# Tokens' sums one chunk sooner, chunk 17's weights ahead of their splits, and the second pair's weight sums later

## The chip, the core and the metric

The kernel runs on one core of one Trainium2 chip. The time is device microseconds of one execution, the median of several runs. TensorE (PE; PEld is its weight load), VectorE (DVE), ScalarE (ACT), GpSimd (POOL) and SyncE (SP, which issues the DMAs) run side by side, each in the order of its own program, and wait for each other at semaphores.

## The reference, cut to what matters

A masked attention feeds a gated mixing block, and that feeds a second mixing block with a channel network. The change lies in the channel network, the last line:

```
x  = attention(q, k, v)                            # 2 x 768 tokens, 512 channels
x  = (u * (w_spatial @ layernorm(v) + b)) @ w_out  # u, v = halves of relu(x @ w_in)
xt = x.transpose(0, 2, 1)
u  = x + (xt @ U @ V).transpose(0, 2, 1)
out = u + relu(u @ w_ch1) @ w_ch2                  # 512 -> 2048 -> 512 channels
```

## The kernel before, in words

Every float32 matrix product is made of three products of rounded halves: a matrix is split in a rounded part (hi) and the rest (lo), and `mm3` (line 238) runs hi x hi, hi x lo, lo x hi. ACT makes hi, POOL or DVE makes lo as source minus hi (`splits`, line 264).

The 2048 hidden channels are 16 chunks of 128. Each chunk is used for two batches of 768 tokens, so there are 32 steps, n = 0 to 31; n = 16 is chunk 0 of batch 1. Chunk n's weights arrive by DMA and are decoded (`ch_decode`, line 841) once, and split again for each use (`ch_split`, line 848) into the tiles wch, in three slots. `m4(n, j)` (line 859) makes the hidden values of half the tokens: 12 matmuls into PSUM bank 0 or 1, then ACT and DVE write them to h as hi and lo, which frees the bank. `m5(n, t)` (line 869) multiplies h by the second weights into the banks 2 to 7, one for each token block; after the last chunk of a batch (n = 15, 31) DVE adds the bank to y and SP sends y out.

For n < 18 one turn of the loop at line 1120 is: 24 matmuls of m4(n), then 18 of m5(n - 1). From n = 18 on, two chunks are taken together in a round of seven products (`m4_seven`, line 977) in place of eight, a Strassen form. It needs sums of token blocks (five of them) and sums of weight blocks (for each pair of chunks):

- `x_sums` (line 913) adds or subtracts blocks of batch 1's tokens: for each of five names and two halves one operation on POOL or DVE and two on DVE, 25 on DVE and 5 on POOL in all. Its results lie in win0, where the DMAs of the chunks' raw weights lay (so the decodes must be over), with bsp as scratch. It is called behind m4(14) (line 1135).
- `x_operands` (line 935) splits these sums into xc: ten roundings on ACT, five subtractions on DVE, five on POOL. Its places held batch 0's tokens, so it is called at n = 16 (line 1123), and its work is forced out at n = 17 (line 1126).
- `w_sums(q)` (line 956) makes pair q's five groups of weight sums and splits them: into wa for even q, into the first halves of wch for odd q.

`m4_seven` runs the products in the order 5, 4, 3, 2, 1, 6, 7 into the banks 0 and 1 in turn. Before a product it forces out the group of weight sums that the product reads, after it come copies and sums on ACT, DVE and POOL (tile tmp), then a share of a list of other steps, mostly m5 of the pair before. In the first round the list holds six m5 of n = 17 and one split of chunk 19's weights.

What fixes the order on the engines is a planner (lines 66 to 190). Work that isn't matrix work is put down as chains of operations (`add`). At each `tick`, called after every three matmuls, the planner goes through the chains in the order in which they were added and emits those operations which, by its own estimate of durations, would start by about the time that TensorE has reached. `flush` emits the rest of the named chains at once, one operation of each in turn. Once emitted, an operation keeps its place on its engine, whatever the true times turn out to be.

Of the kernel before, what the change touches and what calls it, by code (L numbers as in the profile page):

```python
# [28 lines left out]
NCH = 16  # L29
# [36 lines left out]
class Plan:  # L66
# [95 lines left out]
    def tick(self, room=ROOM):  # L162
        now, more, count = self.free["T"], True, dict.fromkeys(LAG, 0)
        while more:
            more = False
            for c in sorted(self.chains, key=lambda c: c.calm):
                key = c.ops[0][0]
                if any(d.ops for d in c.after) or self.free[key] > now + (CALM if c.calm else room):
                    continue
                if self.most and count[key] >= self.most:  # L170
                    continue
                self.probing = 0.0
                c.ops[0][1]()
                start, self.probing = self.probing, None
                if start <= max(now, self.free[key]) + (STALL if room == ROOM else room):
                    count[key] += 1
                    self.emit(c)
                    more = True

    def flush(self, chains):  # L180

        want = list(chains)
        while any(c.ops for c in want):
            for c in [c for c in want if c.ops]:
                first = [d for d in c.after if d.ops]
                if first:
                    want += [d for d in first if d not in want]
                else:
                    self.emit(c)
# [3 lines left out]
def kernel(ctx: ExitStack, tc: tile.TileContext, qk, qt, kn, vab, vn_, gl_,  # L193
# [5 lines left out]
    def program(dense):  # L199
        with tc.tile_pool(name="sb", bufs=1) as sb, \  # L200
                tc.tile_pool(name="ps", bufs=1, space=bass.MemoryType.PSUM) as pp, \
                tc.manual_schedule():
            body(dense, sb, pp)

    def body(dense, sb, pp):
        plan = Plan(nc)
        V, A, G, T, SP = plan.V, plan.A, plan.G, plan.T, plan.SP
        tick, flush = plan.tick, plan.flush
        KEY = {V: "V", A: "A", G: "G", SP: "SP"}

        def tl(tag, n, name):
            t = sb.tile([128, n], F32, tag=tag, name=f"{name}_{int(dense)}")
            plan.home[t.tensor.name] = tag
            return t
# [49 lines left out]
        def splits(hi, lo, src, eh, el):  # L264
            return [o_rnd(eh, hi, src), o_sub(el, lo, src, hi)]
# [390 lines left out]
        P = {}  # L656
# [182 lines left out]
        decoded, split = {}, {}  # L839

        def ch_decode(c):
            f_place(c)
            f, rw = P["f"][c], P["raw"][c % 2]
            ld = plan.add([o_dma(rw.bitcast(I32), w_ch[c].bitcast(I32))], decoded.get(c - 2, []))
            decoded[c] = [plan.add(decode(rw[:, 1024 * j:1024 * j + 1024], f[:, 512 * j:512 * j + 512]), [ld])
                          for j in range(2)]

        def ch_split(n, js=(0, 1)):
            c = seq[n][1]
            w = [t[:, n % 3] for t in P["wch"]]  # L850
            split[n] = [plan.add(splits(w[0][:, 512 * j:512 * j + 512], w[1][:, 512 * j:512 * j + 512],
                                        P["f"][c][:, 512 * j:512 * j + 512], A, G), [decoded[c][j]])
                        for j in js]
# [5 lines left out]
        def m4(n, j, bk):  # L859
            b, c = seq[n]  # L860
            c1, _ = chv(n)
            for k in range(KB):
                mm3(bk[:, 0:384], [c1[l][:, k] for l in range(2)],
                    [X[b][l][:, k, 384 * j:384 * j + 384] for l in range(2)], k == 0, k == KB - 1)
            hi, lo = (P["h1"][n % 2][l][:, 384 * j:384 * j + 384] for l in range(2))
            A.activation(out=r_(hi), in_=bk[:, 0:384], func=AF.Relu)
            V.scalar_tensor_tensor(out=r_(lo), in0=bk[:, 0:384], scalar=0.0, in1=hi, op0=ALU.max, op1=ALU.subtract)
# [15 lines left out]
        def use(n, t, new):  # L883
            if new:
                flush(split[n])
            m5(n, t)
# [3 lines left out]
        SEVEN = NCH + 2  # L890
# [6 lines left out]
        def o_tt(eng, o_, a, b_, op):  # L897
            return KEY[eng], lambda: eng.tensor_tensor(out=o_, in0=a, in1=b_, op=op)
# [36 lines left out]
        def x_operands(two, tmp_):  # L935
            P["xb"] = {"2": [xblock(1, 0, 0)[l] for l in range(2)], "5": [xblock(1, 1, 1)[l] for l in range(2)]}
            places = [t[:, 1536 * n:1536 * n + 1536] for t in (tl("x00", KB * S, "xc0"), tl("x01", KB * S, "xc1"))
                      for n in range(2)] + [tl("uv", 2 * S, "xc2")]
            ready = []
            for p, (c, name) in zip(places, zip(two, ("4", "3", "1", "6", "7"))):  # L940
                hi, lo = (p[:, 768 * l:768 * l + 768].rearrange("p (k t) -> p k t", k=2) for l in range(2))
                P["xb"][name] = [hi, lo]
                ready.append(plan.add([op for k in range(2) for op in splits(hi[:, k], lo[:, k], tmp_[name][k], A, (V, G)[k])],
                                      [c]))
            return ready


        def wblocks(q):
            if q % 2 == 0:
                return [[P["wa"][l][:, 256 * i:256 * i + 256] for i in range(7)] for l in range(2)]  # L950
            return [[P["wch"][l][:, i // 2, 256 * (i % 2):256 * (i % 2) + 256] for i in range(6)]
                    + [P["wa"][l][:, 1792:2048]] for l in range(2)]
# [3 lines left out]
        def w_sums(q, before):  # L956
            n0 = SEVEN + 2 * q
            f0, f1 = (P["f"][seq[n][1]] for n in (n0, n0 + 1))
            a11, a12, a21, a22 = f0[:, 0:256], f0[:, 256:512], f1[:, 0:256], f1[:, 256:512]
            t0, t1_, t2_ = bsp[:, 0:512], P["wk"], bsp[:, 512:768]  # L960
            hi, lo = wblocks(q)

            def two(i):

                return [(wa[:, 256 * i:256 * i + 512] if q % 2 == 0 else wc[:, i // 2, 0:512])
                        for wa, wc in zip(P["wa"], P["wch"])]

            return [plan.add(ops, before[i:i + 1]) for i, ops in enumerate((
                [o_tt(V, t0[:, 0:256], a21, a22, ALU.add), o_tt(V, t0[:, 256:512], a11, a12, ALU.add)]
                + splits(*two(0), t0, A, G),  # L970
                splits(hi[6], lo[6], a22, A, G),
                splits(hi[5], lo[5], a11, A, G),
                [o_tt(V, t1_[:, 0:256], a11, a22, ALU.add), o_tt(V, t1_[:, 256:512], a12, a22, ALU.subtract)]
                + splits(*two(2), t1_, A, G),
                [o_tt(V, t2_, a21, a11, ALU.subtract)] + splits(hi[4], lo[4], t2_, A, G)))]
# [144 lines left out]
        for n in range(1, SEVEN):  # L1120
            if 1 < n and n + 2 < NCH:
                ch_decode(n + 2)
            if n == NCH:
                ready = x_operands(two, tmp_)
            if n == SEVEN - 1:
                flush(ready)
                P["wa"] = [tl(f"win0{l}", 2048, f"wa{l}") for l in range(2)]
                ws = w_sums(0, [])
            if n >= 2:
                flush(split[n])  # L1130
                m4(n, 0, bank[0])
                tick()
                m4(n, 1, bank[1])
                tick()
            if n == NCH - 2:
                flush(decoded[NCH - 1] + decoded[NCH - 2])
                two, tmp_ = x_sums()
            if n + 1 < SEVEN:
                ch_split(n + 1)
            for t in range(NB):  # L1140
                m5(n - 1, t)
                tick()
        P["ht"], P["tmp"] = P["h1t"], tl(T_VN[0][0], N_VN, "tmp")
        steps = [(lambda t=t: m5(SEVEN - 1, t)) for t in range(NB)]
        for n in range(SEVEN, 2 * NCH, 2):
            q, wait = (n - SEVEN) // 2, {i: ws[k:k + 1] for k, i in enumerate((0, 1, 2, 4, 5))}
            ch_split(n, (1,))

            steps.insert(6, lambda n=n: ch_split(n + 1, (1,)))
            if n + 2 < 2 * NCH:  # L1150
                ws = w_sums(q + 1, ws)
            m4_seven(q, wait, steps)
            steps = [(lambda n=n + e, t=3 * j + i, new=(j, i) == (USE[2 * e][1], 0): use(n, t, new))
                     for e, j in USE for i in range(3)]
# [62 lines left out]
```

## Time and profile before

| | |
|---|---|
| median of 3 runs | 540.13 us (539.19 to 540.87) |
| profiled execution, its own time | 540.65 us |
| its span, from first to last instruction | 538.8 us |
| mean granted TensorE clock | 0.981 of 2.4 GHz |
| busy in the span: PE, PEld | 504.5 us (94%), 444.7 us (83%) |
| busy in the span: DVE, ACT, POOL | 382.7 us (71%), 233.7 us (43%), 220.2 us (41%) |

Busy time alone doesn't say where the time goes. The views used below are the chain of waits (what ended last, followed back), the timeline of one engine (start, duration, operation, and in brackets the idle time before it with what ended it), and windows (busy time of each engine in a stretch, with the granted clock). In the rows all operations have the line L56, that of the helper which records them, so they are told apart by the tile that they write and those that they read: h, xsum, xc, wch, wa, tmp, bsp, f. Operations of one kind in a row are merged, with their count behind an x.

### The profile page before, as it was taken

The numbers are of one execution on the slowest core, as the hardware profiler recorded it, in microseconds if no ns is written. First come the engines' busy times: TensorE is split into PE (matmuls) and PEld (weight loads), VectorE is DVE, ScalarE is ACT, GpSimd is POOL, SyncE is SP. The second block draws the span as 40 slices with busy tenths as digits, with TensorE's granted clock in tenths as the row PEclk, the third lists the DMA queues.
The fourth block names the chain that finished last, engine by engine and source line by source line (L and its number), as shares of the span: only waits on it lengthen the run. The fifth ranks groups of instructions, "written<-read, shape, count | busy, mean of one in ns | idle before, by whom it ended". The sixth has DMA issues, their size and how long they took to land.

```text
span 538.8 us, 8155 instructions
## 1 busy us (share of the span) xinstructions
PE 504.5 (94%) x2874; PEld 444.7 (83%) x2874; DVE 382.7 (71%) x848; ACT 233.7 (43%) x565; POOL 220.2 (41%) x245
## 2 busy tenths in 40 slices
PE   5777999799999999999999999999969899999994
PEld 4566877689899999888998998989958788888883
DVE  8896789854599733696898776773998666665443
ACT  4867788521454203564534334243324434444220
POOL 5576556510246103220044233243666556654410
PEclk9988999999999999999999999999989899999998
DMA  8548463300321202321035334210011000000003
GB/s 304 210 134 277 136 213 111 119 2 0 120 77 55 60 0 93 118 104 54 25 97 215 104 131 156 84 74 0 1 65 52 2 1 1 0 1 0 1 1 122
DMA packets 13520, 44.74 MB, mean 83 GB/s; under 512 B 1568, under 2 KB 3744, under 8 KB 11424
## 3 DMA queue, kind: packets, MB, share of 16 engines
q1 hardware_dynamic: 13328, 44.14, 24.2%
q8 instruction: 24, 0.39, 0.3%
q14 instruction: 24, 0.20, 0.1%
q10 hardware_dynamic: 144, 0.00, 0.0%
HBM read 40.99 MB, written 3.15 MB: 82 GB/s over the span
## 4 chain that ended last, share of the span: by engine, by line
PE 81%; DVE 10%; ACT 3%; DMA 2%; issue 2%; POOL 1%; SPq 0%; ACTq 0%; DVEq 0%
PE bank L56 81%; DVE xsum L56 3%; DVE prob L56 2%; DMA stg<-in_w_sp_dram 1%; ACT prob L56 1%; DVE sm L56 1%; DVE rawin L56 1%; DVE y L56 1%; DVE bsp L56 1%; DMA ni<-in_gl_dram 1%; DVE bias L56 1%; ACT vn L56 0%; DVE masks L56 0%; ACT ptb L56 0%; DVE ptb L56 0%
## 5 line engine op out<-in xcount | busy, mean ns | idle before, releaser
L56 PE MATMUL bank<-wch,h 128*128 128x512 f32 x576 | 145.7, 397 | 0.0
L56 POOL TENSOR_TENSOR wch<-f,wch 128x512 fp32r<-128x512 f32 (+1 forms) x56 | 77.5, 1399 | 155.1 <-ACT wch L56 152.6
L56 PEld LDWEIGHTS bank<-wch,h 128*128 128x128 f32 x576 | 107.7, 189 | 20.4
L56 PE MATMUL bank<-x,wch 128*128 128x384 f32 x468 | 88.4, 343 | 5.3 <-ACT wch L56 4.1
L56 PEld LDWEIGHTS bank<-x,wch 128*128 128x128 f32 x468 | 84.1, 192 | 8.7 <-ACT wch L56 4.5
L56 POOL TENSOR_SCALAR prob<-prob,sm 128x232 f32<-128x232 f32 (+1 forms) x96 | 47.1, 508 | 32.7 <-ACT prob L56 25.4
L56 PE MATMUL bank<-wsp,vn 128*128 128x384 f32 x288 | 53.2, 339 | 0.9 <-DVE vn L56 0.4
L56 ACT ACTIVATE prob<-prob,sm 128x232 f32<-128x232 f32 (+1 forms) x96 | 44.4, 464 | 21.4 <-DVE sm L56 21.4
L56 ACT ACTIVATE h<-bank 128x384 fp32r<-128x384 f32 x36 | 17.7, 491 | 78.8 <-PE bank L56 78.8
L56 PEld LDWEIGHTS bank<-wsp,vn 128*128 128x128 f32 x288 | 49.5, 188 | 2.0 <-DVE vn L56 0.7
L56 DVE TENSOR_SCALAR f<-f 128x512 f32<-128x512 f32 (+1 forms) x64 | 41.3, 681 | 9.5 <-ACT f L56 9.3
L56 DVE SCALAR_TENSOR_TENSOR f<-raw,f 128x512 int32<-128x512 int32 x64 | 43.8, 724 | 0.1
L56 DVE TENSOR_TENSOR tmp<-bank,tmp 128x384 f32<-128x384 f32 x42 | 22.6, 552 | 29.9 <-PE bank L56 29.9
L56 PE MATMUL bank<-ident,prob 128*128 128x128 f32 (+1 forms) x176 | 28.9, 288 | 13.3 <-ACT ptb L56 6.0
L56 PE MATMUL bank<-win,x 128*128 128x512 f32 x144 | 40.4, 416 | 0.0
L56 PEld LDWEIGHTS bank<-ident,prob 128*128 128x128 f32 (+1 forms) x176 | 20.2, 140 | 22.9 <-POOL prob L56 13.5
L56 DVE SCALAR_TENSOR_TENSOR h<-bank,h 128x384 fp32r<-128x384 f32 x36 | 19.8, 551 | 23.6 <-ACT h L56 23.6
L56 ACT ACTIVATE h<-tmp 128x384 fp32r<-128x384 f32 x28 | 14.7, 524 | 49.6 <-DVE tmp L56 34.8
L56 PE MATMUL bank<-wo,x 128*128 128x512 f32 x144 | 35.3, 395 | 0.0
L56 ACT ACTIVATE wch<-f 128x512 fp32r<-128x512 f32 (+1 forms) x56 | 32.5, 610 | 3.3 <-DVE f L56 3.3
L56 PE MATMUL bank<-x,win 128*128 128x384 f32 x192 | 33.6, 336 | 0.0
L56 PEld LDWEIGHTS bank<-x,win 128*128 128x128 f32 x192 | 33.3, 188 | 0.1
(116 smaller groups left out, 816.2 us busy)
## 6 DMA issues: line engine op xcount, KB each, us to landing
raw<-in_w_ch_dram SPq DMA_DIRECT2D x16, 1024.0 KB, 4.8
raw<-in_qk_dram SPq DMA_DIRECT2D x20, 360.0 KB, 4.1
vals<-in_vab_dram SPq DMA_DIRECT2D x10, 512.0 KB, 4.3
out_dram<-y SPq DMA_DIRECT2D x12, 256.0 KB, 2.3
stg<-in_w_in_dram SPq DMA_DIRECT2D x5, 512.0 KB, 5.0
stg<-in_w_sp_dram SPq DMA_DIRECT2D x3, 768.0 KB, 5.6
stg<-in_w_out_dram SPq DMA_DIRECT2D x4, 512.0 KB, 3.8
raw<-in_qk_dram SPq DMA_DIRECT2D x4, 256.0 KB, 3.4
```

Source lines behind the costliest of these rows:

```text
L56: return f(*a, **kw)
```

## The change

Three places of the main program change. `x_sums` is called behind m4(13) instead of m4(14), and the decodes of chunks 14 and 15 are forced out there. At n = 17 one flush takes chunk 17's splits together with the tokens' splits, the former first in turn; before, the tokens' splits were flushed alone, and chunk 17's just ahead of m4(17). In the first seven-product round `w_sums(1)` is put in the list of steps as the fifth of now eight steps, so that it is added behind the fifth product; before, it was added ahead of the round. The other pairs' sums are added ahead of the round as before.

```diff
@@ -1123,7 +1123,7 @@
             if n == NCH:
                 ready = x_operands(two, tmp_)
             if n == SEVEN - 1:
-                flush(ready)
+                flush(split[n] + ready)
                 P["wa"] = [tl(f"win0{l}", 2048, f"wa{l}") for l in range(2)]
                 ws = w_sums(0, [])
             if n >= 2:
@@ -1132,7 +1132,7 @@
                 tick()
                 m4(n, 1, bank[1])
                 tick()
-            if n == NCH - 2:
+            if n == NCH - 3:
                 flush(decoded[NCH - 1] + decoded[NCH - 2])
                 two, tmp_ = x_sums()
             if n + 1 < SEVEN:
@@ -1143,12 +1143,16 @@
         P["ht"], P["tmp"] = P["h1t"], tl(T_VN[0][0], N_VN, "tmp")
         steps = [(lambda t=t: m5(SEVEN - 1, t)) for t in range(NB)]
         for n in range(SEVEN, 2 * NCH, 2):
-            q, wait = (n - SEVEN) // 2, {i: ws[k:k + 1] for k, i in enumerate((0, 1, 2, 4, 5))}
+            q = (n - SEVEN) // 2
+            wait = {i: (P["ws"][q] if q else ws)[k:k + 1] for k, i in enumerate((0, 1, 2, 4, 5))}
             ch_split(n, (1,))
 
             steps.insert(6, lambda n=n: ch_split(n + 1, (1,)))
-            if n + 2 < 2 * NCH:
-                ws = w_sums(q + 1, ws)
+            if q == 0:
+                steps.insert(4, lambda: P["ws"].append(w_sums(1, P["ws"][0])))
+                P["ws"] = [ws]
+            elif n + 2 < 2 * NCH:
+                P["ws"].append(w_sums(q + 1, P["ws"][q]))
             m4_seven(q, wait, steps)
             steps = [(lambda n=n + e, t=3 * j + i, new=(j, i) == (USE[2 * e][1], 0): use(n, t, new))
                      for e, j in USE for i in range(3)]
```

## Rows read from the trace of the kernel before

**Rows 1.** Chain of waits, 360 to 432 us: start, us, what

```profile
398.96 0.53 ACT xc L56
...
416.94 0.72 DVE f L56
```

**Rows 2.** Timeline of weight loads (PEld): start, us, operation, idle before

```profile
387.63 4.24 PEld L56 LDWEIGHTS bank<-x,wch 128*128 128x128 f32 x24
391.85 4.09 PEld L56 LDWEIGHTS bank<-wch,h 128*128 128x128 f32 x18
400.43 0.50 PEld L56 LDWEIGHTS bank<-x,wch 128*128 128x128 f32 x2 [4.49 <-ACT wch L56]
402.03 5.60 PEld L56 LDWEIGHTS bank<-x,wch 128*128 128x128 f32 x22 [1.10 <-POOL wch L56]
407.62 4.09 PEld L56 LDWEIGHTS bank<-wch,h 128*128 128x128 f32 x18
411.76 0.42 PEld L56 LDWEIGHTS bank<-x,wa 128*128 128x128 f32 x2
412.43 0.65 PEld L56 LDWEIGHTS bank<-x,wa 128*128 128x128 f32 x4 [0.26 <-POOL wa L56]
...
419.41 1.57 PEld L56 LDWEIGHTS bank<-x,wa 128*128 128x128 f32 x6 [2.26 <-ACT tmp L56]
...
422.14 1.58 PEld L56 LDWEIGHTS bank<-xc,wa 128*128 128x128 f32 x6
...
424.35 1.13 PEld L56 LDWEIGHTS bank<-xc,wa 128*128 128x128 f32 x6
...
426.11 1.13 PEld L56 LDWEIGHTS bank<-xc,wa 128*128 128x128 f32 x6
428.22 0.99 PEld L56 LDWEIGHTS bank<-x,wch 128*128 128x128 f32 x6 [0.98 <-DVE tmp L56]
```

**Rows 3.** Windows of 2 us: length, busy of PE, PEld, DVE, ACT, POOL, clock, DMA

```profile
400.00:402.00 2.00, 1.01 (x2) 0.50 (x2) 2.00 (x4) 0.90 (x2) 2.00 (x3) 0.50 0.03 10
...
420.00:422.00 2.00, 2.00 (x7) 1.90 (x7) 1.15 (x2) 0.15 (x1) 2.00 (x3) 0.50 0.00 0
...
428.00:430.00 2.00, 1.78 (x9) 1.69 (x10) 2.00 (x4) 1.74 (x5) 1.46 (x2) 1.00 0.00 0
```

**Rows 4.** Windows of 20 us, same columns

```profile
380.00:400.00 20.00, 16.38 (x82) 14.40 (x81) 19.80 (x27) 6.67 (x15) 12.06 (x10) 0.98 0.00 1
...
480.00:500.00 20.00, 20.00 (x101) 17.94 (x100) 12.09 (x21) 8.51 (x20) 13.11 (x12) 1.00 0.00 0
```

**Rows 5.** Timeline of DVE

```profile
363.42 2.48 DVE L56 SCALAR_TENSOR_TENSOR f<-raw,f 128x512 int32<-128x512 int32 x4
...
367.61 0.56 DVE L56 SCALAR_TENSOR_TENSOR h<-bank,h 128x384 fp32r<-128x384 f32 x1 [1.24 <-ACT h L56]
...
376.47 0.55 DVE L56 TENSOR_TENSOR xsum<-x 128x384 f32<-128x384 f32 x1
377.12 1.48 DVE L56 TENSOR_TENSOR xsum<-xsum,bsp 128x384 f32<-128x384 f32 x1
...
397.92 0.54 DVE L56 SCALAR_TENSOR_TENSOR h<-bank,h 128x384 fp32r<-128x384 f32 x1
...
408.99 1.22 DVE L56 TENSOR_TENSOR bsp<-f 128x256 f32<-128x256 f32 x2
...
412.42 2.37 DVE L56 TENSOR_TENSOR bsp<-f 128x256 f32<-128x256 f32 x2 [1.20 <-POOL wa L56]
```

**Rows 6.** Timeline of POOL

```profile
368.17 2.57 POOL L56 TENSOR_TENSOR wch<-f,wch 128x512 fp32r<-128x512 f32 x2 [5.63 <-ACT wch L56]
370.70 1.01 POOL L56 TENSOR_TENSOR bsp<-x 128x384 f32<-128x384 f32 x1
...
411.02 1.36 POOL L56 TENSOR_TENSOR wa<-bsp,wa 128x512 fp32r<-128x512 f32 x1 [1.42 <-ACT wa L56]
...
415.91 1.48 POOL L56 TENSOR_TENSOR wch<-bsp,wch 128x512 fp32r<-128x512 f32 x1
```

## The prediction

> **What bounds the kernel now.** Late in the program TensorE works without a break, 20.00 of 20 us between 480 and 500, but only 16.38 between 380 and 400 [rows 4]; a change pays only where it closes such a gap or raises the clock. The chain of waits says why: in the stretch around the change it leaves matrix work twice, first through the sums of the tokens on DVE and their rounding on ACT (the reader sees a rounding of an x sum stand in it), then through a weight sum on DVE [rows 1]. The timeline of the weight loads gives both holes their size [rows 2].
>
> Hole one: m5 of chunk 15 begins at 391.85. A whole m5 takes 411.76 - 407.62 = 4.14 us, so m4 of chunk 17 could begin at 395.99, m5 of chunk 16 one m4 later (391.85 - 387.63 = 4.22) at 400.21, and the first seven-product round at 404.35. It begins at 411.76: 7.41 us lost, 4.44 of them waiting for ACT's rounding of chunk 17, 1.10 for POOL's rest of it, and most of what is left at a granted clock of 0.50, the 1.2 GHz level [rows 3].
>
> Hole two: the first round holds seven products and six m5 blocks. A product and the m5 behind it take 426.11 - 424.35 = 1.76 us, a last product 1.13; 6 x 1.76 + 1.13 = 11.69. It takes 428.22 - 411.76 = 16.46, so 4.77 us are lost: 2.26 waiting for ACT's copy of product 4 (queued behind roundings of the second pair's weight sums that wait for DVE), 0.98 at the end for bank 0, 0.26 at the start for the first weight sum, and 1.42 at the low clock: the pair at 419.41 takes 2.73 instead of 1.76, the product at 422.14 1.58 instead of 1.13. A gap of 0.98 leaves the clock at 1.00, behind one of 2.26 it is 0.50 [rows 3].
>
> Both holes together are 12.18 us. That is the most this change can give back: nothing else in it shortens TensorE's own work.
>
> **The change part by part.** No instruction is added or removed, no DMA is moved past another; what changes is the order on DVE, ACT and POOL.
>
> The tokens' sums are 25 tensor operations on DVE and 5 on POOL. Their first one now runs at 376.47, directly behind the second h of chunk 14 [rows 5]. One chunk sooner it stands behind the second h of chunk 13, which ends at 367.61 + 0.56 = 368.17: 8.3 us sooner. DVE is free there (before its next h it waits). The forced end of the decodes of chunks 14 and 15 costs nothing: the last of them runs at 363.42 to 365.90 [rows 5], in DVE's order before both h of chunk 13. POOL's first sum runs as soon as POOL is free, as it does now at 370.70 [rows 6], then beside a decode; at most its 1.01 us is put on that decode, and h of chunk 13 has time.
>
> What is late next: DVE's backlog holds h, and an h that is late holds the PSUM bank of the next m4. Between 376.47 and 397.92 DVE starts 19 operations of the sums, 2 h and 3 xc subtractions; POOL runs 4 wch subtractions (1.29 each), 4 sums and 3 xc (some 1.01 each) [rows 5, 6]. Added one behind the other: 24 x 0.55 + 5.2 + 7.1 = 25.5 us, and they took 21.45, 0.84 of it. In the new order I count, before the first h of chunk 15, 20 operations of the sums and 3 h on DVE, and 6 wch and 3 sums on POOL: 23 x 0.55 + 7.7 + 3.0 = 23.4 us, times 0.84 is 19.7. So this h starts at 387.9 and ends at 388.4, where m4 of chunk 16 wants its bank at 387.63 [rows 2]: a hold of 0.7 us. Ends of this cost: 0 if two operations less stand ahead of it; 391.5 + 0.55 - 387.63 = 4.4 us, plus 1.4 for the clock, if nothing overlaps. I take the measured overlap, because the operations and their neighbours are the same.
>
> The row on DVE bears on one rule. The same sum takes 0.55 us at 376.47 and 1.48 beside a POOL subtraction in the row after it [rows 5]. The Trainium skill (SBUF — State Buffer, section "Who interferes with whom") says that a DVE instruction with two SBUF inputs and a GpSimd instruction that reads SBUF block each other for the whole instruction. By the rule everything adds up and the 4.4 us hold is the result; by the row only 0.84 of the sum is paid.
>
> After that h, five operations of the sums are left, at some 1 us each beside POOL with one h: the last sum is there near 393.5. ACT's roundings (0.53 each [rows 1]) follow at once, chunk 17's roundings at 394 to 395, its POOL part from 395.3 to 396.6 in the first half. m4 of chunk 17 now wants the first at 396.0 + 0.7, and the POOL part two matmuls later. I take 0; ends 0 and 2 us. Should more be queued, writing chunk 17's chains ahead of those of the sums takes at most the 4.44 us wait away, which is already counted. The six y sums and their output DMAs come in the same place and move forward with it. At the start of the first round the weight sums follow h of chunk 17 as now: I keep the 0.26 us.
>
> The second pair's weight sums now go out after the fifth product. ACT's copy of product 4 then has no such rounding ahead: hole two's 2.26 and 1.42 go. The list behind the products has eight steps instead of seven, so the last m5 falls behind the seventh product, between it and the next round's first product, which shares bank 0: the 0.98 goes too. The price is at the start of the second round. The fifth product ends 5 x 1.13 + 4 x 0.63 = 8.2 us after the round's start; DVE's two operations on it need 2 x 0.55 [rows 5], so the weight sum starts at 9.3. For the first pair the same work took from 408.99 to 411.02 + 1.36 = 3.39 us [rows 5, 6]: 12.7. The second round begins at 11.7 and needs the POOL part two matmuls (0.37) later, at 12.05: a hold of 0.65 us, in which all of TensorE's round stands behind the waiting product. Ends: 0, and with the second pair's present duration (412.42 to 415.91 + 1.48, 4.97 us [rows 5, 6]) 2.2 plus 1.4 for the clock. The later parts have 2 to 8 us more.
>
> Sum: 12.18 - 0.7 - 0.26 - 0.65 = 10.57 us. The profiled execution took 540.65 (span 538.8 and 1.85 around it): 530.1. It lies 0.52 above the median of the three runs, so against that median I predict 529.6 us.
>
> **The rivals.**
> - A, the DVE backlog holds bank 0 of chunk 16: the hold is 4.4 + 1.4 instead of 0.7, so 534.7. For it: DVE is busy for 19.80 of 20 us between 380 and 400 now [rows 4]. Against: the measured overlap. The Trainium skill's rule of the two engines (SBUF — State Buffer, "Who interferes with whom"), taken fully, is this case.
> - B, the second pair's weight sums come late: 2.2 + 1.4 instead of 0.65, so 532.6; with a second late part of the same size 536.2. For it: their present duration. Against: that duration was stretched by the first pair's sums, still on POOL at the time.
> - C, the change doesn't reach hole one, since the planner still puts chunk 17's roundings behind late sums: only hole two closes, 540.13 - 4.77 + 0.65 = 536.0. Against: the sums' ready work starts no sooner than chunk 16, but eight us of DVE work are out of its way.
> - D, slower: the second pair's sums go over into round two, push the third pair's, and so on, and each round begins late by 2.2 + 1.4 = 3.6 us. From three late rounds (10.57 / 3.6 = 2.9) the gain is gone; with four it is 529.6 + 14.4 = 544.0. Against: later rounds keep TensorE at 20.00 of 20 us while POOL has 13.11 and DVE 12.09 [rows 4], so a backlog is worked off within a round.
>
> **How the numbers follow.** Forecast 0.62 (its own range 528 to 532), A 0.12, B 0.12, C 0.05, D 0.05; 0.04 is left for an outcome within what a measurement can tell from no change, 0.3% or 1.6 us. Faster is the first four, 0.91; same 0.04; slower 0.05. The range goes from the floor, 540.13 - 12.18 = 528.0 with 0.4 for the runs' spread, so 527.6, to 536.2, the far end of B, and leaves out D and the rest.
>
> **What would show it.** Right: the weight loads of chunk 17's m4 begin within 1 us of the end of chunk 15's m5 and run at a clock of 1.00; the first round takes under 12.2 us; no ACT wait for wch is left among TensorE's waits, and a short wait on an h or a POOL part stands in its place. The first x sum starts near 368. Wrong: a gap of over 2 us before m4 of chunk 15, 16 or 17, which falsifies the backlog's size, or before the second or third round, which falsifies the price of the late weight sums; each with a granted clock of 0.50 behind it.

## The result and the profile after

The changed kernel takes 533.57 us, median of 16 runs (532.05 to 538.69), against 540.13 before (16 runs): 6.6 us less, ratio 0.9892 with a 95% interval of 0.9868 to 0.9915. (This ratio is not the quotient of the two medians, which is 0.9879; by the ratio the gain is 5.8 us.) The predicted direction and range (527.6 to 536.2) hold; the predicted 529.6 was 4.0 us too low, and the time lies outside the forecast's own range of 528 to 532. The profiled execution took 533.49 us, span 531.7.

Timeline of the weight loads after, over the same stretch as [rows 2]:

```profile
386.72 4.24 PEld L56 LDWEIGHTS bank<-x,wch 128*128 128x128 f32 x24
390.94 4.09 PEld L56 LDWEIGHTS bank<-wch,h 128*128 128x128 f32 x18
397.79 0.30 PEld L56 LDWEIGHTS bank<-x,wch 128*128 128x128 f32 x2 [2.75 <-ACT wa L56]
398.42 5.27 PEld L56 LDWEIGHTS bank<-x,wch 128*128 128x128 f32 x22 [0.33 <-POOL wch L56]
403.68 4.09 PEld L56 LDWEIGHTS bank<-wch,h 128*128 128x128 f32 x18
407.82 1.12 PEld L56 LDWEIGHTS bank<-x,wa 128*128 128x128 f32 x6
...
420.63 0.30 PEld L56 LDWEIGHTS bank<-x,wch 128*128 128x128 f32 x2 [1.33 <-ACT wch L56]
421.24 0.65 PEld L56 LDWEIGHTS bank<-x,wch 128*128 128x128 f32 x4 [0.32 <-POOL wch L56]
...
429.78 0.99 PEld L56 LDWEIGHTS bank<-xc,wch 128*128 128x128 f32 x6 [0.65 <-ACT tmp L56]
```

The same sums as for before. Hole one: a full pace from 390.94 would start the first round at 390.94 + 4.14 + 4.22 + 4.14 = 403.44; it starts at 407.82, so 4.4 us are still lost (7.41 before): 2.7 in front of m4 of chunk 17, and 403.68 - 397.79 = 5.89 instead of 4.22 us in it. Hole two: from 407.82 to the end of the second round's first product, 421.89, are 14.07 us; full pace is 11.69 + 1.12. So 1.26 are lost (4.77 before). The stretch from the m5 of chunk 15 to that product's end is the yardstick for all kernels below. It measures 428.22 + 0.99 - 391.85 = 37.36 before [rows 2] and 421.89 - 390.94 = 30.95 after: 6.4 us, close to the 6.6 us between the medians. It leaves out one later wait, the 0.65 us at 429.78 in the second round: all kernels here with `w_sums(1)` as the fifth step have it (0.65 to 0.70), the others don't. The rest of the 7.1 us between the two spans is not the change's: m5 of chunk 15 already begins 0.9 us sooner, and up to the first sum the order of all instructions is the same.

The clock behind the first hole (windows after; last columns clock, DMA share, GB/s, as in [rows 3]):

```profile
398.00:400.00 2.00, 1.99 (x7) 1.67 (x7) 2.00 (x5) 0.03 (x1) 2.00 (x3) 0.58 0.19 74
400.00:402.00 2.00, 2.00 (x9) 2.00 (x8) 2.00 (x5) 0.03 (x1) 1.01 (x2) 0.57 1.06 408
```

What DVE, POOL and ACT did meanwhile, after, in this order (the first two answer to [rows 5] and [rows 6]):

```profile
366.70 0.56 DVE L56 SCALAR_TENSOR_TENSOR h<-bank,h 128x384 fp32r<-128x384 f32 x1 [0.42 <-ACT h L56]
367.18 0.55 DVE L56 TENSOR_TENSOR xsum<-x 128x384 f32<-128x384 f32 x1
...
385.06 0.54 DVE L56 SCALAR_TENSOR_TENSOR h<-bank,h 128x384 fp32r<-128x384 f32 x1
...
390.69 6.52 DVE L56 TENSOR_TENSOR xc<-xsum,xc 128x384 fp32r<-128x384 f32 x5
397.13 1.01 DVE L56 SCALAR_TENSOR_TENSOR h<-bank,h 128x384 fp32r<-128x384 f32 x2
...
412.85 0.56 DVE L56 TENSOR_TENSOR tmp<-bank,tmp 128x384 f32<-128x384 f32 x1 [7.66 <-PE bank L56]
```

```profile
390.29 6.50 POOL L56 TENSOR_TENSOR xc<-xsum,xc 128x384 fp32r<-128x384 f32 x5 [2.40 <-ACT xc L56]
396.75 2.86 POOL L56 TENSOR_TENSOR wch<-f,wch 128x512 fp32r<-128x512 f32 x2
```

```profile
392.51 1.15 ACT L56 ACTIVATE wch<-f 128x512 fp32r<-128x512 f32 x2
```

The first x sum starts 9.3 us sooner on the trace's scale and the first h of chunk 15 is there at 385.6, 1.1 us before m4 of chunk 16 wants the bank. But both h of chunk 16 stand behind five xc subtractions on DVE; five more run on POOL at the same time, and each pair takes 1.30 us. The first h ends near 397.65, and m4 of chunk 17 starts at 397.79. Chunk 17's own weights don't hold this start: ACT's rounding of them is done at 392.51 + 1.15 = 393.66, and POOL's part is first read by the third matmul, which has a wait of its own (0.33 us).

### The profile page after: what moved, and what is told of

It reads as the page before. It is cut to its first block, busy times and chain, and to the rows that moved or that the text cites. A ratio compares the mean times of both kernels' runs of the same rounds, so it can differ in the third digit from the quotient of the medians.

```text
span 531.7 us, 8160 instructions
## 1 busy us (share of the span) xinstructions
PE 501.2 (94%) x2874; PEld 441.8 (83%) x2874; DVE 383.2 (72%) x848; ACT 233.3 (44%) x565; POOL 221.8 (42%) x245
## 4 chain that ended last, share of the span: by engine, by line
PE 74%; DVE 16%; ACT 6%; issue 2%; DMA 1%; POOL 0%; ACTq 0%; DVEq 0%
PE bank L56 74%; DVE xsum L56 3%; DVE prob L56 2%; ACT prob L56 2%; DVE sm L56 2%; DVE xc L56 1%; DVE bsp L56 1%; DVE h L56 1%; ACT ptb L56 1%; DVE y L56 1%; DVE ptb L56 1%; DVE masks L56 1%; DMA ni<-in_gl_dram 1%; DVE rawin L56 1%; DVE bias L56 1%
## 5 line engine op out<-in xcount | busy, mean ns | idle before, releaser
L56 PE MATMUL bank<-win,x 128*128 128x512 f32 x144 | 39.2, 406 | 0.0
L56 PE MATMUL bank<-raw 64*128 64x232 f32 (+1 forms) x192 | 26.1, 418 | 6.1 <-DMA raw<-in_qk_dram 6.1
```

Source lines behind the costliest of these rows:

```text
L56: return f(*a, **kw)
```

## The experiments

Each kernel was timed beside runs of the kernel before on the same chip; the ratio is to those. The stretch is that defined above, from the kernel's own profile.

| kernel | median us | ratio to before (95%) | stretch us |
|---|---|---|---|
| changed, again | 534.05 | 0.9897 (0.986 to 0.9935) | 30.91 |
| sums alone | 532.99 | 0.9894 (0.985 to 0.9937) | 30.58 |
| weights alone | 538.39 | 0.9984 (0.996 to 1.0008) | 34.92 |
| subtractions on DVE | 530.96 | 0.9845 (0.9809 to 0.9882) | 27.57 |
| first weight sums later | 533.47 (one run) | none | 30.52 |
| h before splits | 532.41 | 0.9862 (0.9806 to 0.9918) | 27.92 |
| DVE and early weights | 528.99 | 0.9801 (0.9767 to 0.9836) | 26.34 |
| all three | 529.15 | 0.9803 (0.9769 to 0.9836) | 26.71 |

The medians of before were 538.78 beside the first four and 540.79 beside the others. The stretch at full pace would be 37.36 - 12.18 = 25.18.

**The changed kernel again.**

> The changed kernel unaltered, as the yardstick of this group: 533.6 us, some 6.5 less than before. Of the two holes of before, 12.18 us, 5.6 should still be lost: 4.4 from the end of m5 of chunk 15 to the first round, 1.25 at the second round.

It came out at 534.05, with the same wait (2.77 us) and the same stretch.

**Sums alone.** The third edit undone:

```diff
-            q = (n - SEVEN) // 2
-            wait = {i: (P["ws"][q] if q else ws)[k:k + 1] for k, i in enumerate((0, 1, 2, 4, 5))}
+            q, wait = (n - SEVEN) // 2, {i: ws[k:k + 1] for k, i in enumerate((0, 1, 2, 4, 5))}
...
-            if q == 0:
-                steps.insert(4, lambda: P["ws"].append(w_sums(1, P["ws"][0])))
-                P["ws"] = [ws]
-            elif n + 2 < 2 * NCH:
-                P["ws"].append(w_sums(q + 1, P["ws"][q]))
+            if n + 2 < 2 * NCH:
+                ws = w_sums(q + 1, ws)
```

> The tokens' sums one chunk sooner, the second pair's weight sums as before. Theory: hole two was a late effect of hole one (DVE and POOL still behind with the tokens' sums), so moving those sums alone also takes ACT's late copy of product 4 away, and only the 0.98 us for bank 0 is left: lost 4.4 + 1.0, some 533.4 us. Rival, that the parts add up: hole two stays at 4.77, 540.13 - 3.03 = 537.1 us.

Weight loads of this kernel, first round:

```profile
407.25 1.12 PEld L56 LDWEIGHTS bank<-x,wa 128*128 128x128 f32 x6
...
410.95 1.00 PEld L56 LDWEIGHTS bank<-xc,wa 128*128 128x128 f32 x6 [0.26 <-ACT tmp L56]
...
419.95 0.99 PEld L56 LDWEIGHTS bank<-x,wch 128*128 128x128 f32 x6 [0.98 <-DVE tmp L56]
```

It is as fast as the full change (0.9894 against 0.9897 on the same chip). The 2.26 us wait for product 4's copy is gone with the early weight sums still in place: DVE, which in the changed kernel has nothing to do for 7.66 us up to product 3, makes them there. Left are the 0.98 for bank 0 and 0.26 for ACT's copy of product 5, which stands behind roundings of these sums. The rival, that the parts add up (537.1), is out.

**Weights alone.** The third edit on top of the kernel before, the other two left out.

> The second pair's weight sums later, the tokens' sums as before. Hole one stays at 7.4 us by both theories. If the late weight sums are what cured hole two, 1.25 us of it are left and the time is 540.13 - 3.5 = 536.6 us; if it was cured by the sooner sums, products 4 to 3 still wait for a DVE that is behind and the time is above 538.5 us.

```profile
390.47 4.09 PEld L56 LDWEIGHTS bank<-wch,h 128*128 128x128 f32 x18
399.04 0.30 PEld L56 LDWEIGHTS bank<-x,wch 128*128 128x128 f32 x2 [4.47 <-ACT wch L56]
400.63 6.40 PEld L56 LDWEIGHTS bank<-x,wch 128*128 128x128 f32 x22 [1.29 <-POOL wch L56]
...
411.15 0.42 PEld L56 LDWEIGHTS bank<-x,wa 128*128 128x128 f32 x2
...
424.13 0.30 PEld L56 LDWEIGHTS bank<-x,wch 128*128 128x128 f32 x2 [1.27 <-ACT wch L56]
424.74 0.65 PEld L56 LDWEIGHTS bank<-x,wch 128*128 128x128 f32 x4 [0.31 <-POOL wch L56]
```

The trace and the timed runs don't quite agree. In the profile hole two shrinks as I had predicted of this edit, to 424.74 + 0.65 - 411.15 = 14.24 us from 17.45, with no wait over 0.3 us inside the round (the 1.27 and 0.31 come at the start of the second one). The stretch is only 2.4 us shorter, because m4 of chunk 17 took 0.8 longer in this execution. The timed runs give 0.9 us (540.13 x 0.9984 = 539.3), at most 2.2: what the second case expected (above 538.5), and clear of the 3.5 of the first. So the edit does cure hole two by itself in the trace, but little of that is seen in the time, which can't be told from no gain. The execution that the trace shows was one of the faster of the twelve (537.16, median 538.39), that of before a slightly slower one (540.65, median 540.13); beyond that, where the rest goes is left open.

**Subtractions on DVE.**

```diff
-    ... splits(hi[:, k], lo[:, k], tmp_[name][k], A, (V, G)[k]) ...
+    ... splits(hi[:, k], lo[:, k], tmp_[name][k], A, V) ...
```

> The changed kernel, with all ten subtractions of the tokens' splits on DVE instead of five on DVE and five on POOL. Theory: DVE and POOL hold each other up, which makes each of the five cost 1.3 us on either engine; eight on DVE alone cost 8 x 0.47 = 3.8 us, so the first h of chunk 16 is there near 395.0 on the scale of the changed kernel's trace, m4 of chunk 17 begins within 0.3 us of the end of the m5 before it, its clock stays at 1.00, and 2.6 + 1.3 us are gained: 529.7 us. Rival, that each subtraction takes DVE 1.3 us by itself or at the pace of ACT's roundings: eight take 10.4 us, h comes at 401, and it is some 3.5 us slower than the changed kernel, 537 us.

Its timelines of weight loads, DVE and POOL:

```profile
389.89 4.09 PEld L56 LDWEIGHTS bank<-wch,h 128*128 128x128 f32 x18
394.03 2.15 PEld L56 LDWEIGHTS bank<-x,wch 128*128 128x128 f32 x12
397.16 2.03 PEld L56 LDWEIGHTS bank<-x,wch 128*128 128x128 f32 x12 [0.98 <-DVE h L56]
...
416.20 0.30 PEld L56 LDWEIGHTS bank<-x,wch 128*128 128x128 f32 x2 [1.29 <-ACT wch L56]
```

```profile
389.64 3.36 DVE L56 TENSOR_TENSOR xc<-xsum,xc 128x384 fp32r<-128x384 f32 x7
392.93 0.54 DVE L56 SCALAR_TENSOR_TENSOR h<-bank,h 128x384 fp32r<-128x384 f32 x1
393.39 3.24 DVE L56 TENSOR_TENSOR xc<-xsum,xc 128x384 fp32r<-128x384 f32 x3
396.56 0.55 DVE L56 SCALAR_TENSOR_TENSOR h<-bank,h 128x384 fp32r<-128x384 f32 x1
```

```profile
392.18 3.57 POOL L56 TENSOR_TENSOR wch<-f,wch 128x512 fp32r<-128x512 f32 x2 [5.33 <-ACT wch L56]
```

Seven subtractions take 3.36 us, 0.48 each, most of it with POOL idle (until 392.18); the last three take 3.24 beside POOL's two. So the first h, with seven subtractions ahead of it instead of five, ends 3.6 us behind the start of m5 of chunk 15 (393.47), against 6.7 in the changed kernel. The last subtraction is not done sooner: it ends 6.7 us behind that start (396.63), against 6.3. m4 of chunk 17 follows the m5 without a gap, at a clock of 1.00, and only its second half waits 0.98 us for the second h, which I had not counted: 530.96 instead of 529.7. The rival (537) is out.

**First weight sums later.**

```diff
                 P["wa"] = [tl(f"win0{l}", 2048, f"wa{l}") for l in range(2)]
-                ws = w_sums(0, [])
             if n >= 2:
@@
                 m4(n, 1, bank[1])
                 tick()
+            if n == SEVEN - 1:
+                ws = w_sums(0, [])
```

> The changed kernel, with the first pair's weight sums added behind m4 of chunk 17 instead of ahead of it. The trace puts the wait before that m4 (2.75 us) down to ACT's rounding of a weight sum (wa). Theory: it was DVE's first h of chunk 16, which frees the bank and ends 0.1 us earlier; so the wait stays at 2.7 us with no wa ahead of it, and the time at 533.6 to 534.5. Rival, that wa is what it waits for: the wait goes and 529.7 us come out.

Weight loads, and then DVE and ACT around the wait:

```profile
397.98 0.30 PEld L56 LDWEIGHTS bank<-x,wch 128*128 128x128 f32 x2 [2.76 <-issue]
398.61 3.77 PEld L56 LDWEIGHTS bank<-x,wch 128*128 128x128 f32 x22 [0.33 <-POOL wch L56]
```

```profile
390.88 6.52 DVE L56 TENSOR_TENSOR xc<-xsum,xc 128x384 fp32r<-128x384 f32 x5
397.32 1.01 DVE L56 SCALAR_TENSOR_TENSOR h<-bank,h 128x384 fp32r<-128x384 f32 x2
```

```profile
403.18 0.72 ACT L56 ACTIVATE wa<-f 128x256 fp32r<-128x256 f32 x2
```

The wait stays at 2.76 us with the first wa 5 us behind it, so the profile's "ACT wa" was the neighbour that ended last, and h was the cause, as the theory had it. That the time agrees too is partly luck: m4 of chunk 17 ran at full clock here and took 1.5 us less than in the changed kernel, and the first weight sums, now late, cost waits of 0.24 and 1.06 us at the first round.

**h before splits.** `x_operands` called behind `ch_split(n + 1)` at n = 16 instead of at the head of the turn:

```diff
-            if n == NCH:
-                ready = x_operands(two, tmp_)
...
                 ch_split(n + 1)
+            if n == NCH:
+                ready = x_operands(two, tmp_)
```

> The changed kernel, with the tokens' splits added behind m4 of chunk 16 and chunk 17's splits instead of ahead of that m4, so that both h of chunk 16 stand ahead of the subtractions on DVE, and chunk 17's part ahead of them on POOL. Theory (the bank is held by h behind the subtractions): m4 of chunk 17 begins without a wait and with the clock at 1.00; the subtractions then run beside it and the first weight sums come up to 0.5 us late: 529.5 to 530.5 us. Rival, that the five subtractions on each engine cost their 6.5 us wherever they stand: the first round begins late by what m4 gained, 532.5 to 534 us.

```profile
395.05 4.23 PEld L56 LDWEIGHTS bank<-x,wch 128*128 128x128 f32 x24
...
403.83 0.30 PEld L56 LDWEIGHTS bank<-x,wa 128*128 128x128 f32 x2 [0.47 <-ACT wa L56]
405.27 0.65 PEld L56 LDWEIGHTS bank<-x,wa 128*128 128x128 f32 x4 [1.15 <-POOL wa L56]
```

The bank's wait is gone by order alone, and m4 runs at full pace. The first weight sums then wait behind the subtractions, 1.6 us instead of the 0.5 at most that I gave them: between theory and rival. The median, 532.41, lies there too, but its four runs spread from 529.09 to 535.25.

**DVE and early weights.** The edit of "subtractions on DVE", and `steps.insert(1, ...)` instead of 4.

> All ten subtractions on DVE, and the second pair's weight sums added behind the second product (step 1 of the list) instead of the fifth; the list keeps its eight steps. Theory: DVE stands idle through the first three products of the first round, so early weight sums cost nothing and the 1.3 us wait at the second round goes; of the rest only the 1 us wait for the second h of chunk 16 is left: 529.6 us if the subtractions alone give 530.9. Rival, that early weight sums are what hurt before: ACT's copies of the products 4 and 3 come late again, 2.3 us and a slow clock behind it, 533 us.

```profile
396.85 2.03 PEld L56 LDWEIGHTS bank<-x,wch 128*128 128x128 f32 x12 [0.97 <-DVE h L56]
...
414.94 0.99 PEld L56 LDWEIGHTS bank<-x,wch 128*128 128x128 f32 x6 [0.39 <-DVE tmp L56]
```

The theory holds in the trace: the waits at the second round fall from 1.29 and 0.31 (subtractions on DVE) to 0.39, for DVE's sum of product 7 in bank 0, and the 0.97 for the second h is left as before. The time, 528.99, is near the expected 529.6, but the intervals of the two ratios (0.9801 and 0.9845) overlap, so the runs alone don't show this step.

**All three.** That, with `x_operands` moved as above.

> The version that the experiments point to: the tokens' splits added behind m4 of chunk 16 and chunk 17's splits, all their subtractions on DVE, the second pair's weight sums at step 1. Theory: neither h of chunk 16 is held, POOL is free for chunk 17, the subtractions lie beside m4 of chunk 17 and no wait over 0.5 us is left up to the second round: 528.2 to 529 us, some 11 us under the kernel before. Rival, that ten subtractions behind the y sums hold the h of chunk 17 and with it the first weight sums: the first round begins 2 us late, 530.5 to 531.5 us.

```profile
395.14 4.23 PEld L56 LDWEIGHTS bank<-x,wch 128*128 128x128 f32 x24
...
405.33 0.65 PEld L56 LDWEIGHTS bank<-x,wa 128*128 128x128 f32 x4 [1.42 <-POOL wa L56]
```

```profile
396.54 4.30 DVE L56 TENSOR_TENSOR xc<-xsum,xc 128x384 fp32r<-128x384 f32 x9
```

It trades the 0.97 us for h against 1.42 for the first weight sums, so the theory's "no wait over 0.5 us" is wrong, and ends level with the version before it, 0.15 us above the theory's range and below the rival's. With POOL idle (its next operation starts at 400.98) nine subtractions take DVE 4.30 us; with the one ahead of them (0.55) ten take 4.85, where five pairs took 6.52 in the changed kernel. Both are some 2% faster than the kernel before and about 1% faster than the changed one.

## Why the prediction was right and where it failed

- The direction was right, and the mechanism in part: of the 12.18 us of both holes 4.4 + 1.26 = 5.6 were left, not the 1.6 that the sum of the prediction leaves. That the time still lies in the stated range is partly luck: the range's upper end came from rival B, not from the wait that was missed. One of the prediction's own signs of being wrong came: a gap of over 2 us (2.75) in front of m4 of chunk 17, with a granted clock of 0.58 behind it.
- The size of the holes, 12.18 us, was right as a ceiling: the best versions come within 1.2 and 1.5 us of the full pace.
- The backlog of DVE ahead of chunk 15's first h was slightly overstated. I put its start at 387.9, 19.7 us behind the end of the h ahead of the first sum; it took 385.06 - (366.70 + 0.56) = 17.8. I had counted one sum and one h too many on DVE, and on POOL two wch subtractions too many and one sum too few. So the 0.7 us hold of chunk 16 (0.8 by the prediction's own 388.4 - 387.63) did not come, nor rival A's 4.4 us there.
- The step that failed is the one behind it, "I take 0; ends 0 and 2 us" for m4 of chunk 17. I followed ACT's roundings and POOL's part of chunk 17, but left out the five xc subtractions that DVE runs between the last sum and both h of chunk 16. They took 6.52 us beside POOL's five. It is the mechanism of rival A, an h that stands behind DVE's backlog and holds the bank, one chunk later than I looked. The term measured 2.7 us of waiting and 1.7 in a slower m4, 4.4 instead of 0: that, less the 0.7 and 0.26 which did not come, is 3.4 of the 4.0 us by which the prediction was off. Subtractions on DVE makes those ahead of the first h shorter, h before splits puts them behind both h, and either removes the wait in front of this m4; with the first weight sums later it stays.
- The measured overlap of 0.84 was right where it could be looked at again: five pairs of subtractions on both engines take 6.52 us, and 5 x (0.55 + 1.01) = 7.8 times 0.84 is 6.55. By the Trainium skill (SBUF — State Buffer, section "Who interferes with whom") the two block each other fully. The rows show nearly that: a pair takes 1.30 us, where full blocking would give the sum of 1.56, and on DVE alone the same subtraction takes 0.48. I had the rule and the figure, and applied both only up to the h of chunk 15.
- The late weight sums cost 1.26 us at the second round, not 0.65: the two sums of its first group run at 417.50 and 418.63 with a product's sum between them, and POOL's part ends at 419.78 + 1.40 = 421.18, 3.68 us behind the first instead of 3.39, and the first starts 0.4 later than I had it. That is the other 0.6 us. The profile puts the first 1.33 us of the wait down to ACT; DVE's sum of product 7, which frees bank 0, ends only at 419.97 + 0.54 = 420.51, behind the weight sums, and may be what ended it (not tested). Nor does the 0.98 us for bank 0 go entirely, as I had it: in DVE and early weights, where no weight sum stands ahead of that operation, 0.39 are left. DVE's and POOL's timelines after show the order:

```profile
417.50 0.74 DVE L56 TENSOR_TENSOR bsp<-f 128x256 f32<-128x256 f32 x1
418.16 0.54 DVE L56 TENSOR_TENSOR tmp<-bank,tmp 128x384 f32<-128x384 f32 x1
418.63 0.41 DVE L56 TENSOR_TENSOR bsp<-f 128x256 f32<-128x256 f32 x1
...
419.97 0.54 DVE L56 TENSOR_TENSOR tmp<-bank,tmp 128x384 f32<-128x384 f32 x1
```

```profile
419.78 1.40 POOL L56 TENSOR_TENSOR wch<-bsp,wch 128x512 fp32r<-128x512 f32 x1 [1.82 <-ACT wch L56]
```

- The credit was given to the wrong edit. I let the third edit repair hole two (2.26, 1.42 and 0.98). Sums alone shows that the first edit repairs all but some 1.0 us of it (waits of 0.98 and 0.26), since its root was the same backlog; weights alone, that in the trace the third edit repairs it too if the first is not there. Together they gain what the first gains alone, as far as the runs can tell (0.9897 and 0.9894). In the sum this did not show, because only one of the two was counted.
- The second edit, the joint flush, does nothing: written the old way, the changed program has the same instructions in the same order on every engine. It was not run. The tokens' splits have all been emitted by then, and chunk 17's stand behind them on ACT (392.51) and on POOL (396.75), not ahead of them as the title has it.
- Rival C's kind of miss came in part (a late queue still in front of m4 of chunk 17), but not by its road: chunk 17's roundings were done at 393.66, before that m4 could have begun (395.08). Of B's 3.6 us 1.26 came; D did not come.

## What to carry to other kernels

When a backlog is moved, follow it to the end of its chain on every engine, and ask at each step which PSUM bank's release stands behind it in the same queue; the wait moves to the first release that I didn't price. Two engines that hold each other up are little help to one another: ten subtractions took 4.85 us on DVE with POOL idle and 6.52 us as five on each, but with POOL at other work beside the last three they were done no sooner. Before crediting a repair to an edit, ask whether the edit ahead of it has already removed the cause; running each alone is what showed it here.

## What was not expected of the hardware

A wait of the same length did not cost the same. Four traces have a wait of 2.75 to 2.78 us in front of m4 of chunk 17. In three of them (the changed kernel twice, and sums alone) this m4 then took 5.84 to 5.89 us, at a granted clock that fell to between 0.50 and 0.63; with the first weight sums later it ran at 1.00 and took 402.36 - 397.98 = 4.38. The window behind the wait, in the changed kernel again, sums alone and first weight sums later, in this order (the changed kernel's first one stands above):

```profile
398.00:400.00 2.00, 1.88 (x6) 1.58 (x7) 2.00 (x4) 0.32 (x2) 2.00 (x3) 0.63 0.03 13
```

```profile
398.00:400.00 2.00, 2.00 (x7) 2.00 (x8) 2.00 (x5) 0.00 (x0) 2.00 (x3) 0.50 0.48 187
```

```profile
398.00:400.00 2.00, 1.98 (x10) 1.67 (x11) 2.00 (x4) 0.00 (x0) 1.81 (x2) 1.00 0.10 38
```

So with the same wait ahead of it the m4 cost some 1.5 us more in three traces, at the lower clock, than in the fourth. Whether that is chance or comes with the order of that kernel, one trace of it can't tell. And the wait in front of m4 of chunk 17 was shown under the wrong engine, with under 0.1 us between the ends of the true one (h) and the one shown (wa): moving the suspected neighbour away settled it.
